# Keys by Strassen's half-size products from the fourth batch on, and their left blocks from DRAM

## The chip, the cores and the metric

The kernel runs on one core of a Trainium2 chip. The metric is the device time of one execution in microseconds; where several executions were timed, it is their median. A trace of one profiled execution of the kernel before is at hand.

## What is computed

Attention of eight batches of eight heads (512 local tokens with a window of 32, 32 global tokens, head size 64) is followed by a feed-forward part on all 576 tokens of a batch:

```python
x_prev = np.concatenate([np.zeros((B, 1, D), dtype=np.float32), x[:, :-1, :]], axis=1)
xk = mu_k * x + (1.0 - mu_k) * x_prev
xr = mu_r * x + (1.0 - mu_r) * x_prev
k = np.maximum(xk @ w_k, 0.0)
v = k * k @ w_v
r = 1.0 / (1.0 + np.exp(-(xr @ w_r)))
return (r * v).astype(np.float32)
```

Here x is the attention's output, of width 512; w_k is 512 x 1024, w_v 1024 x 512 and w_r 512 x 512, all in fp32. The three products are called keys, values and gates below.

## The kernel before, in words

Every fp32 matrix of the feed-forward part is split into a high and a low part, and a product of two matrices is made of three matmuls (high by high, high by low, low by high), written in `products` (L483 to L485). A matmul here has 128 x 128 weights and 256 columns. The low part of a split is made by a subtraction on POOL or DVE (L202, L517), the high part by a cast on ACT (L201, L516).

A batch has two halves of 256 tokens. For each, `mix` makes xk and xr (L508 to L517), `squares` makes keys and their squares: four groups of 24 matmuls, each into one bank, a relu on ACT (L549) and a multiplication on DVE (L551). `gates` makes the gates (L564, L566).

From batch 2 on (`FROM`), the values are made by Strassen's method for the two halves together: k squared is cut into four blocks B11, B12, B21, B22; `differences` makes T1 to T4 of them on DVE (L620); and seven half-size products take the place of eight (`values_1`, `values_2`, `product`, matmuls at L639). Their left blocks, parts of w_v and sums of them, lie in DRAM (`scratch`): `sums_of_values` makes them during batch 1 (stores at L231 and L245, additions and subtractions on POOL at L232 to L240), and `load_left` (L258) loads them into five buffers, two loads of 512 KB after each product of 24 matmuls. Sums of products are put together by copies of a bank on ACT (L657, L664, L674) and additions on DVE (L660, L673, L678, L685). The keys' weights wk_h and wk_l stay in SBUF all the time.

The heads' attention of the next batch runs beside the feed-forward steps of this one (`together`, `beside_heads`). Head scores are matmuls at L346 and L350, the softmax is L318 (DVE), L324 (ACT) and L334 (POOL), probabilities are transposed on TensorE (L371) and copied from PSUM at L373, by ACT for e = 0 and by DVE for e = 1. Nothing runs beside batch 7's feed-forward part and that of the global tokens: this is called the tail. The order of instructions on each engine is made by a scheduler when the kernel is built, from the order of the code, priorities and its own estimates; on the chip each engine and each queue then works strictly in that order. SP issues all DMA transfers, in order too.

The accumulators take PSUM banks in turn:

```python
MIDDLE_USE = {"m": [ps2, ps2, psx], "s": [ps4] * 4, "t": [ps1], "o": "s"}
```

## Time and profile before

| what | number |
|---|---|
| median of 3 runs | 703.33 us (700.31 to 703.79) |
| the profiled execution's own time | 702.47 us |
| its span in the trace | 700.6 us |
| mean granted TensorE clock | 0.978 |
| HBM read and written | 104.86 MB and 17.30 MB |
| loads of 768 KB of queries and keys, of 640 KB of v | 32 and 32 |

The profile's page gives busy time by engine, a view by stage gives it between two times, and a list of waits says what an idle engine was released by. Two lines of the page's slices, each a fortieth of the span, show how much of the start differs from the rest:

```profile
PE   4879989988999999999999999999999999999997
DMA  8732579462312452362909083635727090534665
```

A digit is the busy share in tenths (9 is 90% or more). Span times start at the first instruction; the batches' boundaries lie about 76 us apart from about 290 us on, and the last heads end at about 596 us.

### The profile page before, as it was taken

To read this page: it belongs to the slowest core of one execution; us is meant where nothing else is said; L and a number is where in the kernel's file an instruction comes from. 1 tells how busy PE (TensorE), PEld (TensorE's weight loads), DVE (VectorE), ACT (ScalarE), POOL (GpSimd) and SP (SyncE) were. 2 spreads that over 40 slices of the span, in tenths; PEclk is the share of its full clock that TensorE was granted. 3 is DMA by queue.
4 is the path that set the end of the run, shared out by engine and by line. 5 is a ranking of instruction groups with operands and counts; after the bars stand their busy time and mean duration, and the time that the engine had idled before them with its cause. 6 is when DMAs were issued, how large, how long until landed. Compare 5 with 4: busy or idle time off the path is not lost.

```text
span 700.6 us, 18622 instructions
## 1 busy us (share of the span) xinstructions
PE 667.4 (95%) x7472; PEld 629.2 (90%) x7472; DVE 417.7 (60%) x1217; ACT 387.9 (55%) x1058; POOL 357.2 (51%) x363
## 2 busy tenths in 40 slices
PE   4879989988999999999999999999999999999997
PEld 2658778978999999999999999999999999999996
DVE  5767977635635375645684557645674656477531
ACT  5756876447445456656557473757465643442530
POOL 5656597864524334573428353645348332642800
PEclk9659999999999999999999999999999999999999
DMA  8732579462312452362909083635727090534665
GB/s 344 288 99 109 200 215 338 157 237 80 127 71 92 132 216 76 122 242 75 359 20 338 25 312 140 222 140 175 279 89 274 2 352 11 196 121 166 216 189 198
DMA packets 43542, 123.37 MB, mean 176 GB/s; under 512 B 4032, under 2 KB 20928, under 8 KB 43456
## 3 DMA queue, kind: packets, MB, share of 16 engines
q1 hardware_dynamic: 43456, 122.18, 49.0%
q8 instruction: 59, 0.97, 0.6%
q14 instruction: 27, 0.22, 0.1%
HBM read 104.86 MB, written 17.30 MB: 174 GB/s over the span
## 4 chain that ended last, share of the span: by engine, by line
PE 75%; DMA 7%; POOL 6%; ACT 5%; DVE 4%; issue 2%; SPq 0%; POOLq 0%; ACTq 0%; DVEq 0%
PE ps_m L639 16%; PE ps_m L483 14%; PE ps_m L484 13%; PE ps_m L485 13%; PE ps_s L350 9%; DMA a<-scratch 3%; PE ps_t L371 3%; ACT Pt L324 2%; PE ps_s L352 2%; DMA w<-w_r 2%; DMA w<-w_v 1%; POOL Pt L334 1%; PE ps_t L421 1%; PE ps_t L350 1%; PE ps_t L380 1%
## 5 line engine op out<-in xcount | busy, mean ns | idle before, releaser
L483 PE MATMUL ps_m<-xkh,wk_h 128*128 128x256 f32 x544 | 155.4, 286 | 4.1 <-ACT xkh L516 2.8
L484 PE MATMUL ps_m<-xkl,wk_h 128*128 128x256 f32 x544 | 154.0, 283 | 0.4 <-POOL xkl L517 0.4
L485 PE MATMUL ps_m<-xkh,wk_l 128*128 128x256 f32 x544 | 153.8, 283 | 0.0
L639 PE MATMUL ps_m<-bh,a 128*128 128x256 f32 x736 | 139.5, 283 | 1.3 <-DMA a<-scratch 1.2
L324 ACT ACTIVATE Pt<-Pt,m 128x160 f32<-128x160 f32 x256 | 106.6, 419 | 26.7 <-DVE m L318 25.0
L639 PEld LDWEIGHTS ps_m<-bh,a 128*128 128x128 f32 x736 | 115.4, 188 | 4.0 <-issue 2.0
L483 PEld LDWEIGHTS ps_m<-xkh,wk_h 128*128 128x128 f32 x544 | 103.8, 191 | 6.1 <-ACT xkh L516 3.4
L334 POOL TENSOR_TENSOR Pt<-Pt,ssum 128x512 f32<-128x512 f32 x64 | 68.6, 1072 | 79.7 <-ACT xrh L516 23.2
L484 PEld LDWEIGHTS ps_m<-xkl,wk_h 128*128 128x128 f32 x544 | 103.9, 191 | 1.3 <-POOL xkl L517 0.7
L485 PEld LDWEIGHTS ps_m<-xkh,wk_l 128*128 128x128 f32 x544 | 103.7, 191 | 0.5 <-issue 0.2
L639 PE MATMUL ps_m<-bl,a 128*128 128x256 f32 x368 | 103.0, 280 | 0.0
L517 POOL TENSOR_TENSOR xkl<-xfull,xkh 128x512 fp32r<-128x512 f32 x34 | 46.9, 1379 | 99.3 <-ACT xkh L516 94.3
L483 PE MATMUL ps_m<-xrh,wr_h 128*128 128x256 f32 x272 | 78.4, 288 | 2.5 <-ACT relu L528 2.5
L551 DVE TENSOR_TENSOR B<-ps_m,relu 128x512 f32<-128x512 f32 x52 | 35.8, 689 | 74.6 <-ACT relu L549 74.5
L484 PE MATMUL ps_m<-xrl,wr_h 128*128 128x256 f32 x272 | 77.4, 285 | 0.0
L485 PE MATMUL ps_m<-xrh,wr_l 128*128 128x256 f32 x272 | 77.3, 284 | 0.0
L549 ACT ACTIVATE relu<-ps_m 128x512 f32<-128x512 f32 x52 | 31.0, 597 | 82.6 <-PE ps_m L485 82.6
L639 PEld LDWEIGHTS ps_m<-bl,a 128*128 128x128 f32 x368 | 69.2, 188 | 0.0
L318 DVE CUSTOM_DVE_ANT_0 Pt<-ps_s,masks 128x160 f32<-128x160 f32 x256 | 65.7, 317 | 2.6 <-PE ps_s L350 2.4
L586 POOL TENSOR_TENSOR gate<-sum,gate 128x512 f32<-128x512 f32 x18 | 26.7, 1481 | 59.3 <-DVE sum L685 38.4
L201 ACT CAST bh<-B 128x512 fp32r<-128x512 f32 x76 | 46.0, 620 | 18.2 <-PE ps_m L639 12.1
L483 PEld LDWEIGHTS ps_m<-xrh,wr_h 128*128 128x128 f32 x272 | 52.2, 192 | 3.2 <-ACT relu L528 2.6
(138 smaller groups left out, 1573.6 us busy)
## 6 DMA issues: line engine op xcount, KB each, us to landing
a<-scratch SPq DMA_DIRECT2D x92, 512.0 KB, 6.2
raw_qk<-qk SPq DMA_DIRECT2D x32, 768.0 KB, 5.5
raw_v<-v SPq DMA_DIRECT2D x32, 640.0 KB, 5.9
out_l<-gate SPq DMA_DIRECT2D x32, 256.0 KB, 4.6
w<-w_k SPq DMA_DIRECT2D x8, 512.0 KB, 9.7
w<-w_v SPq DMA_DIRECT2D x8, 512.0 KB, 4.5
w<-w_r SPq DMA_DIRECT2D x4, 512.0 KB, 4.0
scratch<-wv_h SPq DMA_DIRECT2D x8, 256.0 KB, 3.2
```

Source lines behind the costliest of these rows:

```text
L201: nc.scalar.copy(hi, val)
L318: read = nc.vector.tensor_tensor_reduce(out=Pt[:, i], in0=place(e, t, h), in1=masks[:, e, slots[t][1]], op0=ALU.add, op1=ALU.min, scale=-s ...
L324: nc.scalar.activation(Pt[:, i], Pt[:, i], AF.Exp, bias=low_x[:, i:i + 1], scale=-1.0, accum_out=ssum[:, i:i + 1],)
L334: nc.gpsimd.tensor_mul(out, Pt[:, each, at:at + n], rinv.unsqueeze(2).to_broadcast([P, 4, n]))
L350: self.last = nc.tensor.matmul(*a, **kw)
L483: nc.tensor.matmul(out, w_h[:, i, cols], x_h(i), start=(i == 0), stop=False)
L484: nc.tensor.matmul(out, w_h[:, i, cols], x_l(i), start=False, stop=False)
L485: nc.tensor.matmul(out, w_l[:, i, cols], x_h(i), start=False, stop=(i == n - 1))
L517: nc.gpsimd.tensor_sub(lo[:, both], xf, hi[:, both].bitcast(F32))
L549: nc.scalar.activation(rk, kp, AF.Relu)
L551: nc.vector.tensor_mul(k2[f0 // HC][f0 % HC // 2], kp, rk)
L639: nc.tensor.matmul(out[:, j], w, x[:, i % 2], start=fresh and (i, j, n) == (0, 0, 0), stop=(i, n) == (HC - 1, 2), skip_group_check=True,)
```

## The change

Keys of batches 3 to 7 are made by Strassen's method as well. `sums_of_keys` makes the left blocks of w_k during batch 2 and stores them in DRAM (`scratch_k`); wk_h and wk_l are then given up, and their room holds the split blocks of xk (`kxp`). The keys of a batch are two sets (n = 0, 1), each a `seven` with products of 12 matmuls and one left load of 512 KB each. `seven` serves keys and values; it takes three banks X, Y and Z and returns to X and Z for later products of the set. `Keys.mixed` makes the blocks T1 to T4 of xk: four subtractions on DVE, seven casts on ACT and seven low parts on POOL for a batch, in place of four casts and four low parts. Six buffers hold left blocks, in the tail six more tiles that the heads no longer use. The left blocks are loaded one by one, after each step of 12 matmuls: 170 loads instead of 92.

The sums of w_v's blocks move from every step of batch 1's feed-forward part to every other step of its second half, and wait for the last square of the batch's keys. The first chunks of weights are loaded into tiles of `mixp` and `gatep` instead of a pool of their own. From the fourth batch of heads on, both copies of transposed probabilities are by ACT (20 copies move). Gates are always evacuated with high priority. The keys of the global tokens are made from left blocks in DRAM too (`keys_of_one`). In the middle the steps beside a batch's heads are counted as 32 instead of 19.

```diff
-    MIDDLE_USE = {"m": [ps2, ps2, psx], "s": [ps4] * 4, "t": [ps1], "o": "s"}
+    MIDDLE_USE = {"m": [psa, psb, psx], "s": [ps4] * 4, "t": [ps1], "o": "s"}
...
+    gatew = ctx.enter_context(tc.tile_pool(name="gatew", bufs=1))
+    wr_h, wr_l = (gatew.tile([P, NC, NC * P], F32R, name=f"wr_{x}") for x in "hl")
+    keyu = ExitStack()
+    keyw = keyu.enter_context(tc.tile_pool(name="keyw", bufs=1, reuse_waits="tile"))
+    wk_h, wk_l = (keyw.tile([P, NC, DF], F32R, name=f"wk_{x}") for x in "hl")
...
+            home, tag = ((mixp, "mix"), (gatep, "gate"))[n // 2] if n < EARLY else (stage, "w64")
...
+    scratch_v = dramp.tile([P, len(LEFT), HC // 2, 2, 2, TOK], F32, name="scratch_v")
+    scratch_k = dramp.tile([P, len(LEFT), 2, 2, 2, TOK], F32, name="scratch_k")
...
+    def sums(home, tag, parts, out, first, after):
+        a = home.tile([P, 2, 2, TOK], F32, tag=tag, name="a")
+        hs, ls = (home.tile([P, 4, TOK], F32R, tag=tag, name=f"{x}s") for x in "hl")
+        for j in range(2):
+            for x in range(2):
+                behind(after, nc.sync.dma_start(out=out(2 * j, 2 * j + 2, x), in_=parts(x, j)))
+            add = first.tensor_add(a[:, j], parts(0, j), parts(1, j))
+            behind(after, add)
+        a11, a21, a12, a22 = (a[:, j, e] for j in range(2) for e in range(2))
...
+    def sums_of_keys():
+        for i in range(2):
+            for s in range(2):
+                sums(
+                    leftp, "a",
+                    lambda x, j: (wk_h, wk_l)[x][:, i + 2 * j].bitcast(F32)
+                    .rearrange("p (e s n) -> p s e n", e=2, s=2)[:, s],
+                    lambda lo, hi, x: scratch_k[:, lo:hi, s, i, x], nc.vector, Tokens.square,
...
+    SEVEN = (("A11", "B11"), ("A12", "B21"), ("S2", "T2"), ("S1", "T1"), ("S3", "T3"), ("S4", "B22"), ("A22", "T4"))
...
+    for b in range(FROM, B - 1):
+        plan(of_values, [a for a, _ in SEVEN])
+        plan(of_keys, [a for a, _ in SEVEN], True)
+    plan(of_keys, FOUR, True)
+    plan(of_values, [a for a, _ in SEVEN])
+    plan(of_values, ("A11", "A21", "A12", "A22"))
...
-        copy = nc.vector.tensor_copy if e else nc.scalar.copy
+        copy = nc.vector.tensor_copy if e and r.slots[0][0].b <= FROM else nc.scalar.copy
...
+                    xf = self.two(tmpp, "xfull") if hi is not None else blocks[c0 // 2]
...
+    def product(out, right, fresh=True):
+        for i, (b_h, b_l) in enumerate(right):
+            a, home = left.pop(0)
+            for c in range(2):
+                for j in range(2):
+                    a_h, a_l = (a[:, c, x, j * P:(j + 1) * P] for x in range(2))
+                    for n, (w, x) in enumerate(((a_h, b_h), (a_h, b_l), (a_l, b_h))):
+                        nc.tensor.matmul(
+                            out[:, j], w, x[:, c], start=fresh and (i, c, j, n) == (0, 0, 0, 0),
+                            stop=(i, c, n) == (len(right) - 1, 1, 2), skip_group_check=True,
+                        )
+            load_left(home)
+            yield
+    def new_bank():
+        return psum("m").rearrange("p (j n) -> p j n", j=2)
+    def seven(right, done):
+        X, Y, Z = new_bank(), new_bank(), new_bank()
+        if len(use["m"]) == 3:
+            turn["m"] -= 2
+        c11, u2, w = (sump.tile([P, 2, TOK], F32, tag="sum", name=name) for name in ("c11", "u2", "w"))
+        def add(bank, sum, *at):
+            with tc.high_priority():
+                nc.vector.tensor_add(sum, bank, sum)
+            done(*at, sum)
+        def copy(sum, bank):
+            with tc.high_priority():
+                nc.scalar.copy(sum, bank)
+        yield from product(X, right("B11"))
+        copy(c11, X)
+        yield from product(Y, right("B21"))
+        add(Y, c11, 0, 0)
+        yield from product(X, right("T2"), fresh=False)
+        copy(u2, X)
+        yield from product(Z, right("T1"))
+        copy(w, Z)
+        yield from product(X, right("T3"), fresh=False)
+        add(X, w, 1, 1)
+        yield from product(Z, right("B22"), fresh=False)
+        add(Z, u2, 0, 1)
+        yield from product(X, right("T4"), fresh=False)
+        done(1, 0, X)
...
+        def mixed(self):
+            B11, B21, B12, B22 = (self.xv[f"B{i}{j}"] for j in (1, 2) for i in (1, 2))
+            self.x_split("B11", B11)
+            self.x_split("B21", B21)
+            nc.vector.tensor_sub(B11, B12, B11)
+            nc.vector.tensor_sub(B12, B22, B12)
+            self.x_split("B22", B22)
+            nc.vector.tensor_sub(B22, B22, B11)
+            self.x_split("T2", B22)
+            self.x_split("T1", B11)
+            nc.vector.tensor_sub(B21, B21, B22)
+            self.x_split("T3", B12)
+            self.x_split("T4", B21)
+        def x_split(self, name, val):
+            self.x[name] = h, l = [Tokens.two(kxp, f"x{name}{x}", F32R, name + x) for x in "hl"]
+            split(val, h, l, nc.gpsimd)
...
+        def keys(self):
+            blocks = {(i, j): self.block(f"B{i + 1}{j + 1}") for j in range(2) for i in range(2)}
+            for n in range(2):
+                def done(i, j, v):
+                    if in_psum(v):
+                        rk = Tokens.two(tmpp, "relu")
+                        with tc.high_priority():
+                            nc.scalar.activation(rk, v, AF.Relu)
+                        with tc.high_priority():
+                            nc.vector.tensor_mul(blocks[i, j][n], v, rk)
+                    else:
+                        nc.vector.scalar_tensor_tensor(blocks[i, j][n], v, 0.0, v, op0=ALU.max, op1=ALU.mult)
+                yield from seven(lambda b: [self.x[b]], done)
...
+        def values(self):
+            def done(i, j, v):
+                self.tokens[j].write(i, v)
+            for n, _ in enumerate(seven(lambda b: self.parts.pop(b), done)):
+                if n == 4:
+                    self.split("T1", "T3", "B22", "T4")
+                yield
...
+        def keys_of_one(self):
+            t, = self.tokens
+            for i in (1, 2):
+                k = att2.tile([P, 8 * WG], F32, tag="Pt", name="k")[:, :HC * TOK]
+                k = k.rearrange("p (i n) -> p i n", n=TOK)
+                self.k[f"B{i}1"] = [k[:, 2 * n:2 * n + 2] for n in range(2)]
+            blocks = [self.k[f"B{i}1"] for i in (1, 2)]
+            halves = [[(t.xk_h[:, c:c + 2], t.xk_l[:, c:c + 2])] for c in (0, 2)]
+            for n in range(2):
+                for e in range(2):
+                    out = new_bank()
+                    yield from product(out, halves[0])
+                    yield from product(out, halves[1], fresh=False)
...
+            sums = sums_of_values()
+            for n, _ in enumerate(feed_forward(tokens_of(b), before)):
+                if n > FF_STEPS and n % 2:
+                    next(sums, None)
...
+                    keyu.close()
+                    kxp = ctx.enter_context(tc.tile_pool(name="kxp", bufs=1, reuse_waits="tile"))
+                    for _ in range(6):
+                        load_left()
...
+        this.mix(0)
+        for n, _ in enumerate(before.values()):
+            yield
+            if n == 4:
+                this.mix(1)
+            if n == 8:
+                this.mixed()
+        yield from this.tokens[0].gates()
+        if b == B - 1:
+            of_globals.tokens[0].mix()
+        yield from this.keys()
+        this.split("B11", "B21")
+        this.differences()
+        this.split("T2")
+        yield from this.tokens[1].gates()
...
+    for home in ((rawp, "qk", K0 + SK), (rawp, "v", NV), (att2, "PT", 8 * P)):
+        for _ in range(2):
+            load_left(home)
...
+        yield from of_globals.keys_of_one()
+        yield from last.values()
+        yield from of_globals.tokens[0].gates()
+        of_globals.split("B11", "B21")
+        yield from of_globals.values_of_one()
```

Three places show how the order of instructions changes. First the start: POOL, around the last two low parts of w_v's chunks (`wv_l`) and what stands between them and batch 1's mixes (`xkl`, `xrl`). Before:

```order
L202 TENSOR_TENSOR wv_l<-w_991,wv_h 128x512 [waits DMAHW7_49,Activation_49]
L232 TENSOR_TENSOR a<-wv_h,wv_l 128x512 [waits Pool_49]
L232 TENSOR_TENSOR a<-wv_h,wv_l 128x512
L334 TENSOR_TENSOR Pt<-Pt,ssum 128x4x128 [waits DVE_49,PE_49,Activation_49]
L334 TENSOR_TENSOR Pgl<-Pt,ssum 128x128 [waits PE_49]
L334 TENSOR_TENSOR Pt<-Pt,ssum 128x4x128 [waits Activation_49]
L334 TENSOR_TENSOR Pgl<-Pt,ssum 128x128
L237 TENSOR_TENSOR a<-a 128x256 [waits Pool_49]
L202 TENSOR_TENSOR wv_l<-w_1000,wv_h 128x512 [waits DMAHW2_49,Activation_49]
L202 TENSOR_TENSOR wv_l<-w_1112,wv_h 128x512 [waits DMAHW5_49,Activation_49]
```

`a` is a tile of sums. Now, from the same low parts on:

```order
L203 TENSOR_TENSOR wv_l<-w_994,wv_h 128x512 [waits DMAHW2_49,Activation_49]
L203 TENSOR_TENSOR wv_l<-w_1003,wv_h 128x512 [waits DMAHW3_49,Activation_49]
L381 TENSOR_TENSOR Pt<-Pt,ssum 128x4x128 [waits DVE_49,PE_49]
L381 TENSOR_TENSOR Pgl<-Pt,ssum 128x128 [waits PE_49]
L381 TENSOR_TENSOR Pt<-Pt,ssum 128x4x128
L381 TENSOR_TENSOR Pgl<-Pt,ssum 128x128
L203 TENSOR_TENSOR wv_l<-w_1115,wv_h 128x512 [waits DMAHW4_49,Activation_49]
L570 TENSOR_TENSOR xkl<-xfull,xkh 128x512 [waits PE_49,Activation_49]
L570 TENSOR_TENSOR xrl<-xfull,xrh 128x512 [waits PE_49,Activation_49]
```

The sums of w_v (now L242 to L249) are gone from this place; they stand further on, behind the last square (`k`) of batch 1's keys.

Second the middle: TensorE in the keys of batch 4. Before, a chain of products with the weights in SBUF, in which the heads' transposes stand:

```order
L483 MATMUL ps_m<-xkh,wk_h 128x256
L484 MATMUL ps_m<-xkl,wk_h 128x256
L485 MATMUL ps_m<-xkh,wk_l 128x256
L371 MATMUL ps_t<-ident,Pt 128x128 [waits Activation_49]
L371 MATMUL ps_t<-ident,Pt 128x128 x3
L483 MATMUL ps_m<-xkh,wk_h 128x256
L484 MATMUL ps_m<-xkl,wk_h 128x256
L485 MATMUL ps_m<-xkh,wk_l 128x256
```

Now, the second half of the product T2 and the start of T3, both in bank X; ACT copies the bank (`u2`) between them, and the first row of T3 waits for ACT (`Activation`):

```order
L649 MATMUL ps_m<-xT2h,a 128x256 x2
L649 MATMUL ps_m<-xT2l,a 128x256
L649 MATMUL ps_m<-xT2h,a 128x256
L649 MATMUL ps_m<-xT1h,a 128x256
L399 MATMUL ps_s<-raw_qk 64x160 [waits DMAHW7_49,DVE_49]
L397 MATMUL ps_s<-raw_qk 64x160 x15
L427 MATMUL ps_t<-ident,Pgl 128x128 [waits Activation_49]
L427 MATMUL ps_t<-ident,Pgl 128x128
L649 MATMUL ps_m<-xT3h,a 128x256 [waits DMAHW1_49,Activation_49]
L649 MATMUL ps_m<-xT3l,a 128x256
```

Between the last matmul of T2 and the first of T3 stand one matmul of T1 and the heads' scores. SP's queue in the same batches, with the loads of left blocks (`a`), of the heads' inputs and the stores of outputs, before:

```order
L258 DMA a<-scratch 128x1024 [waits DMAHW7_49,PE_49]
L710 DMA out_l<-gate 128x2x256 [waits DMAHW0_49,Activation_49,Pool_49]
L258 DMA a<-scratch 128x1024 [waits DMAHW1_49,PE_49]
L258 DMA a<-scratch 128x1024 [waits DMAHW4_49,DMAHW2_49,PE_49]
L710 DMA out_l<-gate 128x2x256 [waits DMAHW3_49,DVE_49]
L258 DMA a<-scratch 128x1024 [waits DMAHW5_49,PE_49]
L258 DMA a<-scratch 128x1024 [waits DMAHW6_49,PE_49]
L710 DMA out_l<-gate 128x2x256 [waits Pool_49]
L269 DMA raw_qk<-qk 128x1536 [waits DMAHW7_49,PE_49]
L269 DMA raw_qk<-qk 128x1536 [waits DMAHW0_49,PE_49]
```

And now:

```order
L305 DMA a<-scratch_v 128x1024 [waits DMAHW0_49,PE_49]
L305 DMA a<-scratch_v 128x1024 [waits DMAHW1_49,PE_49]
L305 DMA a<-scratch_v 128x1024 [waits DMAHW4_49,DMAHW2_49,PE_49]
L305 DMA a<-scratch_v 128x1024 [waits DMAHW5_49,DMAHW3_49,PE_49]
L305 DMA a<-scratch_v 128x1024 [waits DMAHW6_49,PE_49]
L316 DMA raw_qk<-qk 128x1536 [waits PE_49] x2
L305 DMA a<-scratch_v 128x1024 [waits DMAHW7_49,PE_49]
L321 DMA raw_v<-v 128x1280 [waits DMAHW0_49,PE_49]
L321 DMA raw_v<-v 128x1280 [waits DMAHW1_49,PE_49]
L305 DMA a<-scratch_v 128x1024 [waits DMAHW2_49,PE_49]
L305 DMA a<-scratch_v 128x1024 [waits DMAHW3_49,PE_49]
```

The heads' inputs stand behind more loads of left blocks, each of which waits for a product (`PE`) to free its buffer.

Third the end of the heads: POOL, from the last `Pg` of the heads on. Now:

```order
L455 TENSOR_SCALAR Pg<-Pg,ssumg 128x576 [waits DVE_49,Activation_49]
L203 TENSOR_TENSOR bl<-T_8759,bh 128x512 [waits PE_49,DVE_49,Activation_49,Pool_49]
L203 TENSOR_TENSOR xB11l<-xB_8842,xB11h 128x512 [waits PE_49,Activation_49]
L570 TENSOR_TENSOR xrl<-xfull,xrh 128x512 [waits Activation_49]
L203 TENSOR_TENSOR bl<-T_8759,bh 128x512 [waits Activation_49]
L203 TENSOR_TENSOR xB21l<-xB_8843,xB21h 128x512 [waits Activation_49]
L570 TENSOR_TENSOR xrl<-xfull,xrh 128x512 [waits Activation_49]
L203 TENSOR_TENSOR bl<-B_8396,bh 128x512 [waits PE_49,Activation_49]
L203 TENSOR_TENSOR bl<-B_8396,bh 128x512 [waits Activation_49]
L570 TENSOR_TENSOR xrl<-xfull,xrh 128x512 [waits Activation_49]
L203 TENSOR_TENSOR xT1l<-xB_8842,xT1h 128x512 [waits Activation_49]
L638 TENSOR_TENSOR gate<-c_8869,gate 128x512 [waits DMAHW4_49,DMAHW0_49,DVE_49]
```

The low parts of xk's blocks (`xB11l` and so on) stand between those of the values' blocks (`bl`) and of xr; before, POOL had the following from the second mix of batch 7 on:

```order
L202 TENSOR_TENSOR bl<-B_8363,bh 128x512 [waits Activation_49,Pool_49]
L202 TENSOR_TENSOR bl<-B_7830,bh 128x512 [waits PE_49,Activation_49]
L586 TENSOR_TENSOR gate<-sum,gate 128x512 [waits DMAHW4_49,DMAHW2_49,DVE_49]
L202 TENSOR_TENSOR bl<-B_7830,bh 128x512 [waits Activation_49]
L202 TENSOR_TENSOR bl<-B_7831,bh 128x512 [waits PE_49,Activation_49]
L517 TENSOR_TENSOR xkl<-xfull,xkh 128x512 [waits PE_49,Activation_49,Pool_49]
L517 TENSOR_TENSOR xrl<-xfull,xrh 128x512 [waits PE_49,Activation_49,Pool_49]
L517 TENSOR_TENSOR xkl<-xfull,xkh 128x512 [waits Activation_49]
L202 TENSOR_TENSOR bl<-B_7831,bh 128x512 [waits Activation_49]
L517 TENSOR_TENSOR xrl<-xfull,xrh 128x512 [waits Activation_49]
```

267 lines of the change are left out of this document (109 added, 158 removed).

## The prediction

> **What bounds the kernel now.** I read the page first: busy time, clock, and the engines' shares of the chain that ended last.
>
> ```profile
> span 700.6 us, 18622 instructions
> PE 667.4 (95%) x7472; PEld 629.2 (90%) x7472; DVE 417.7 (60%) x1217; ACT 387.9 (55%) x1058; POOL 357.2 (51%) x363
> PE 75%; DMA 7%; POOL 6%; ACT 5%; DVE 4%; issue 2%; SPq 0%; POOLq 0%; ACTq 0%; DVEq 0%
> ```
>
> TensorE is busy for 95% of the span, and the chain is mostly TensorE. An average hides stages, so the second view is busy time by stage, and the third the list of what TensorE waited for after 165 us.
>
> ```profile
> 165.00:240.00 75.00, 75.00 (x884) 71.22 (x884) 37.65 (x131) 40.38 (x120) 31.99 (x34) 1.00 0.25 89
> 408.00:484.00 76.00, 76.00 (x905) 72.97 (x902) 46.68 (x145) 44.82 (x127) 39.08 (x39) 1.00 0.52 190
> 484.00:560.00 76.00, 75.51 (x898) 72.60 (x898) 46.64 (x145) 44.74 (x127) 38.34 (x38) 1.00 0.48 173
> 596.00:648.00 52.00, 52.00 (x450) 51.97 (x448) 33.72 (x49) 22.29 (x40) 24.47 (x18) 1.00 0.48 162
> PE ps_m L639 <- DMA a<-scratch: 1.2, 3, 0.5
> ```
>
> The columns are length, busy time of PE, weight load, DVE, ACT and POOL, then clock, DMA share and GB/s. From 165 us on TensorE has no gap but 1.2 us; the middle batches repeat every 76 us with 47, 45 and 39 us of work on the other three engines. So here fewer matmuls are time, one for one, as long as nothing new makes TensorE wait.
>
> **Term 1: matmuls that go.** The keys of a batch were 192 matmuls of 256 columns (64 at each of L483, L484 and L485) and become two sets of seven products of 12, 168. Five batches change: 120 matmuls fewer. A matmul's listed 283 ns is its latency; what counts is the distance of starts, from these rows.
>
> ```profile
> 421.30 0.28 PE L483 MATMUL ps_m<-xkh,wk_h 128*128 128x256 f32 x1
> 423.92 0.28 PE L485 MATMUL ps_m<-xkh,wk_l 128*128 128x256 f32 x1
> 399.39 0.28 PE L483 MATMUL ps_m<-xrh,wr_h 128*128 128x256 f32 x1
> 401.78 0.28 PE L485 MATMUL ps_m<-xrh,wr_l 128*128 128x256 f32 x1
> 647.92 5.61 PE ps_m L639 x48
> ```
>
> The keys' first and last start enclose 23 distances: 2.62 / 23 = 0.1139 us. The gates' enclose 20: 2.39 / 20 = 0.1195. The products of the values take 5.61 / 48 = 0.1169. With keys at 0.1139 and the new products at 0.1169 a batch saves 21.87 − 19.64 = 2.23 us; with both at 0.1169, 2.81; with the new ones at the gates' pitch, 21.87 − 20.08 = 1.79. I take 2.5, five times: **−12.5 us**, between −9 and −14. The change does make the matmuls fewer: the order of the engine's instructions has 3816 of this form where it had 3936, and no other kind changes in number. That rules out the rival that it doesn't do what it says (702.5 us).
>
> **Term 2: the start.** The sums of the left blocks of w_v leave the stretch in which TensorE still waits.
>
> ```profile
> 115.00:120.00 5.00, 3.60 (x31) 3.37 (x30) 4.70 (x6) 1.15 (x4) 5.00 (x7) 1.00 0.96 313
> 145.00:150.00 5.00, 4.11 (x64) 3.36 (x62) 3.84 (x19) 3.40 (x16) 3.89 (x4) 1.00 0.75 258
> 150.00:155.00 5.00, 4.38 (x93) 4.07 (x97) 1.63 (x11) 0.87 (x2) 4.57 (x8) 1.00 0.97 320
> 155.00:160.00 5.00, 2.41 (x40) 1.78 (x40) 3.53 (x8) 2.56 (x6) 0.36 (x1) 1.00 1.00 379
> 160.00:165.00 5.00, 4.25 (x23) 4.04 (x24) 2.50 (x17) 4.89 (x20) 2.51 (x2) 0.71 0.29 102
> 161.89 0.42 PE L484 MATMUL ps_m<-xkl,wk_h 128*128 128x256 f32 x1
> 165.10 0.41 PE L484 MATMUL ps_m<-xkl,wk_h 128*128 128x256 f32 x1
> 153.26 0.69 POOL a L239
> 155.39 1.05 ACT hs L242
> ```
>
> From 145 to 165 us TensorE is idle for 0.89 + 0.62 + 2.59 + 0.75 = 4.85 us, and 15 distances in 3.21 us (0.214 us each) cost 15 × (0.214 − 0.114) = 1.5 us more; at 115 to 120 us 1.4 us are idle. On the chain lie POOL's sums and ACT's copy of them. Removing all would give 4.85 + 1.5 + 1.4 = 7.8 us. But the heads' own softmax chain comes next, and the other order of the first batches may cost as much as the windows above show in one place, 2.6 us. I take **−3 us**, range −7 to +3. The sums then run between about 165 and 240 us and those of the keys behind them, where POOL has 32 us of work in 75: nothing for them. The first chunks of weights in other tiles, and the copies of probabilities on ACT instead of DVE (below), are also at nothing.
>
> **Term 3: what the new form adds beside TensorE.** Rows by group:
>
> ```profile
> L373 DVE COPY PT<-ps_t 128x512 f32<-128x512 f32 x32 | 21.9, 685 | 25.3 <-PE ps_t L371 25.3
> L373 ACT COPY PT<-ps_t 128x512 f32<-128x512 f32 x32 | 18.8, 588 | 7.8 <-PE ps_t L371 7.8
> L620 DVE TENSOR_TENSOR B<-B,B 128x512 f32<-128x512 f32 x24 | 19.9, 829 | 0.2
> L685 DVE TENSOR_TENSOR sum<-ps_m,sum 128x512 f32<-128x512 f32 x6 | 4.1, 689 | 1.6 <-PE ps_m L639 1.4
> L551 DVE TENSOR_TENSOR B<-ps_m,relu 128x512 f32<-128x512 f32 x52 | 35.8, 689 | 74.6 <-ACT relu L549 74.5
> L549 ACT ACTIVATE relu<-ps_m 128x512 f32<-128x512 f32 x52 | 31.0, 597 | 82.6 <-PE ps_m L485 82.6
> L201 ACT CAST bh<-B 128x512 fp32r<-128x512 f32 x76 | 46.0, 620 | 18.2 <-PE ps_m L639 12.1 <-DVE B L551 3.5 <-POOL gate L586 1.5
> L202 POOL TENSOR_TENSOR bl<-B,bh 128x512 fp32r<-128x512 f32 x36 | 47.0, 1323 | 2.5 <-ACT bh L201 2.5
> L517 POOL TENSOR_TENSOR xkl<-xfull,xkh 128x512 fp32r<-128x512 f32 x34 | 46.9, 1379 | 99.3 <-ACT xkh L516 94.3 <-issue 5.0
> ```
>
> For a middle batch: DVE loses 4 copies (−2.7 us), 8 squares (−5.5) and L673's add (−0.7), and gains 4 differences (3.3), 6 adds and 8 squares of the two sets (9.6): 46.7 + 4.0 = 51 of 73.5 us. ACT gains 4 copies (2.4), 7 casts for 4 (1.9), 6 evacuations (3.5) and loses 6 relus (−3.6): 49 of 73.5. POOL gains 7 low parts for 4, 7 × 1.32 − 4 × 1.38 = 3.7: 43 of 73.5. None becomes the bound, so their sums cost nothing; their delays might.
>
> *Banks.* A product now goes back into a bank that a copy or add has just left: X, then Y or Z, then X again, four times in a set of seven, eight times a batch for keys, 40 in all. (In the values' sets the product between has 24 matmuls.) For keys it has 12: 12 × 0.1169 = 1.40 us, against 0.588 us for ACT's copy or 0.689 for DVE's add. The tightest place in the order (T3 behind T2) has not a whole product between, only one matmul and small head products. The evacuations are ahead of the rest by priority, yet must let the running instruction end (0.83 us for a difference). A wait is so between 0 and 0.689 + 0.83 + 0.23 − 1.40 = 0.35 us a time, with two matmul distances for the handover: 0 to 14 us in all. The old order's waits of this kind, the squares' among them, cost nothing after 165 us, so I stay near that end: **+2**.
>
> *Left blocks.* Each step of 12 matmuls now takes a 512 KB load; a middle batch has 28 instead of 14.
>
> ```profile
> a<-scratch SPq DMA_DIRECT2D x92, 512.0 KB, 6.2
> DMA to landing us min/median/max: 3.4/6.2/8.4
> 484.75 8.30 DMA a<-scratch
> 405.00:410.00 5.00, 5.00 (x107) 4.81 (x104) 0.89 (x7) 3.88 (x9) 5.00 (x7) 1.00 0.89 342
> 410.00:415.00 5.00, 5.00 (x66) 4.64 (x65) 3.82 (x5) 2.89 (x6) 2.26 (x3) 1.00 0.97 331
> 415.00:420.00 5.00, 5.00 (x43) 4.91 (x43) 3.91 (x20) 3.48 (x16) 1.21 (x1) 1.00 1.02 396
> 420.00:425.00 5.00, 5.00 (x46) 5.00 (x45) 2.27 (x6) 2.52 (x8) 2.74 (x3) 1.00 1.01 360
> 100.00:105.00 5.00, 3.06 (x21) 2.33 (x22) 3.11 (x6) 3.54 (x7) 3.68 (x4) 1.00 1.01 274
> ```
>
> Now 190 GB/s over 76 us are 14.4 MB a batch; 14 loads more are 7.3 MB, 21.8 in all. The four saturated rows average 357 GB/s, so the queue needs 61 of 73.5 us: busy, but not the bound. Six buffers give a load about five steps of 73.5 / 28 = 2.6 us, 13 us, against 6.2 to 8.4 for landing; behind heads' loads on SP's queue some have less. The old kernel paid 1.2 us for such cases; I take **+1.5**, from 0 to 6. In the tail a step of 1.40 us asks 374 GB/s, just over those rows, but gates and six more homes lie between: in the same term. At the heads' end POOL has 19 low parts nearly in a row, 19 × 1.32 = 25 us, which 28 steps of 1.40 us use one by one: **+0.5** (0 to 4).
>
> **Sum.** The profiled execution took 702.47 us (span 700.6): 702.5 − 12.5 − 3 + 2 + 1.5 + 0.5 = 691.0. The median of the runs shown is 703.33, 0.9 above it, and their range of 3.5 us is wider than that, so no correction.
>
> **A rule against it.** The row at 155 to 165 us shows what idling costs: TensorE busy for 2.41 of 5 us, then the clock 0.71. The next row shows a shorter wait that did no harm.
>
> ```profile
> 490.00:495.00 5.00, 4.51 (x52) 4.08 (x45) 4.23 (x21) 2.81 (x13) 1.77 (x1) 1.00 1.01 383
> ```
>
> The Trainium skill, "TensorE: Matmul & The Clock Gate", section "HAM oscillation — how this bites in real kernels", says that a slice of compute shorter than the wait for the next slice's data drops the clock at each slice, and "A second HAM failure mode: psum-queue depth-cycling" says the same of many short idles between groups that cycle through banks. By the first rule the time would be that of rival D. The trace agrees only for the long idle; half a microsecond at 493 us left the clock at 1.00.
>
> **Rivals.** A: *the start gains fully and no new wait appears*: 702.5 − 14 − 7 = 681.5. For it: no such wait cost anything after 165 us. Against: the rings are fuller than before.
> B: *ScalarE's and VectorE's copies hold the banks*: 40 times 0.35 us, 702.5 − 12.5 − 3 + 14 + 1.5 + 0.5 = 703. For it: both engines are two thirds busy, and one product is all the cover. Against: the mean evacuation is half of that cover.
> C, the slower side: *the loads pace the middle batches.* If the queues hold not 357 but the 274 GB/s of the row at 100 us, a batch takes 21.8 / 0.274 = 79.5 us instead of 76: four batches +14, and the tail's 58 loads (30.4 MB, some 29 after the ring's first) 106 us, 2 over the 104 that it has now: 702.5 − 3 + 14 + 2 = 715.5. It decides once the rate falls under 21.8 / 76 = 287 GB/s. Against: that row is of loads of weights among others; those of left blocks run at 331 to 396.
> D: *waits as long as at 155 us come once in each of ten sets*, 2.5 us idle and 1.5 for the clock: 691 + 40 = 731. It needs loads that land 2.5 us later than their cover.
>
> **Chances.** The forecast with its own bounds (685 to 698) 0.66, A 0.12, B 0.12 (two thirds of it within 0.5%), C 0.08, D 0.02. A measurement of this kernel can tell about 0.5% (3.5 us) from no change. Faster: 0.66 + 0.12 = 0.78, within: 0.09, slower: 0.13. The range leaves out a good half of A below and most of C and D with the upper part of B above: 683 to 703.
>
> **What would show it.** Right: starts of key products 0.114 to 0.120 us apart; the middle batches at 73 to 74 us; after 200 us waits of TensorE on ACT or DVE below 3 us and on loads below 3; DMA share about 0.8 in the middle; no sums of w_v on POOL ahead of 160 us and fewer idle microseconds there. Wrong: waits for ps_m's evacuations in every set (B), a DMA share of 1.0 with TensorE idle before each product (C), a clock under 1.00 after 200 us (D), or a start that ends later than 165 us.

## The result and the profile after

The changed kernel took 748.73 us (median of 4 runs, 747.78 to 750.29) beside 702.96 us for the kernel before (4 runs, 700.31 to 703.79): a ratio of 1.066, 95% interval 1.0625 to 1.0695. It is slower by 46 us; 12 us less had been forecast.

The page of the changed kernel, first its span, its busy times, the granted clock by slices and the engines' shares of the chain:

```profile
span 747.3 us, 18702 instructions
PE 684.1 (92%) x7352; PEld 638.0 (85%) x7352; DVE 496.0 (66%) x1249; ACT 406.3 (54%) x1097; POOL 418.1 (56%) x398
PEclk9659889999999999999997999979997999989999
PE 60%; DVE 21%; POOL 6%; ACT 6%; issue 4%; DMA 2%; SPq 0%; POOLq 0%; ACTq 0%; DVEq 0%
```

TensorE has 120 matmuls fewer and is busy longer. DVE's share of the chain went from 4% to 21%, and DVE is busy for 78 us more where the prediction had added 4 us a batch. The clock falls in slices far behind the start.

To see where, both spans are cut at the same points of the heads' work (starts of DVE's copies into xg_all, of which a batch's heads have two): batches 0 and 1, batch 2's feed-forward part with the sums, the four middle batches, the tail. Busy times by stage, the kernel before and then the changed one (length, then PE, PEld, DVE, ACT, POOL, clock, DMA share, GB/s):

```profile
0.00:226.90 226.90, 198.94 (x2241) 175.71 (x2243) 145.66 (x463) 138.36 (x401) 140.97 (x166) 0.93 0.51 181
226.90:297.70 70.80, 70.80 (x858) 67.27 (x855) 41.06 (x141) 40.30 (x119) 28.05 (x29) 1.00 0.38 137
297.70:594.10 296.40, 295.83 (x3494) 285.16 (x3492) 178.39 (x539) 170.13 (x470) 145.70 (x138) 1.00 0.50 181
594.10:700.60 106.50, 101.80 (x901) 101.04 (x897) 52.56 (x77) 39.15 (x68) 42.47 (x31) 1.00 0.54 178
```

```profile
0.00:225.80 225.80, 205.57 (x2240) 181.94 (x2241) 145.20 (x462) 137.44 (x400) 138.24 (x158) 0.90 0.50 177
225.80:312.00 86.20, 78.91 (x882) 73.90 (x880) 58.97 (x150) 48.36 (x131) 57.29 (x57) 0.96 0.72 246
312.00:633.70 321.70, 296.79 (x3384) 279.92 (x3383) 227.68 (x557) 178.44 (x494) 169.22 (x147) 0.95 0.76 257
633.70:747.30 113.60, 102.80 (x863) 102.27 (x859) 64.12 (x82) 42.10 (x73) 53.33 (x39) 0.95 0.71 253
```

The first stage is 1 us shorter, the second 15.4 longer, the middle 25.3, the tail 7.1. The cuts do not hold quite the same work: of the matmuls into ps_m 26 more lie ahead of the middle than before, the middle has 140 fewer where 96 go, the tail 6 fewer where 24 go. At 0.117 us each, some 3 us of the second stage's 15.4 are work that came later before (an estimate). What TensorE waited for behind 165 us (the line that waited, what released it, us in total, times, longest):

```profile
PE ps_t L418 <- ACT PTg L428: 12.1, 4, 6.8
PE ps_m L530 <- DVE c L669: 9.0, 2, 5.4
PE ps_m L649 <- ACT u L674: 6.9, 1, 6.9
PE ps_t L418 <- ACT PT L420: 3.5, 1, 3.5
PE ps_s L399 <- DVE xT L519: 2.7, 1, 2.7
PE ps_m L649 <- POOL bl L203: 2.6, 1, 2.6
PE ps_m L649 <- DMA a<-scratch_k: 1.2, 1, 1.2
```

Few waits, each long: near the start of each middle batch and of the tail lies a hole of one wait or two, 3.0, 6.8, 6.9, 7.0 and 6.9 us. Loads cost 1.2 us. The waits of 3.5 and 2.7 us lie in the second stage. The one at 399 us, engine by engine (start, duration, engine, line; in brackets the idle time before and its releaser), shows how it comes about:

```profile
390.07 0.48 DVE L563 SCALAR_TENSOR_TENSOR xfull<-diff,mu_r_sb,xT 128x256 f32<-128x256 f32 x1
391.14 1.53 DVE L563 SCALAR_TENSOR_TENSOR xB<-diff,mu_k_sb,xT 128x256 f32<-128x256 f32 x1
394.04 2.95 DVE L563 SCALAR_TENSOR_TENSOR xB<-diff,mu_k_sb,xT 128x256 f32<-128x256 f32 x2
396.91 2.93 DVE L563 SCALAR_TENSOR_TENSOR xfull<-diff,mu_r_sb,xT 128x256 f32<-128x256 f32 x2
400.37 0.68 DVE L669 TENSOR_TENSOR c<-ps_m,c 128x512 f32<-128x512 f32 x1
404.11 0.31 DVE L365 CUSTOM_DVE_ANT_0 Pt<-ps_s,masks 128x160 f32<-128x160 f32 x1
```

```profile
390.87 1.51 POOL L203 TENSOR_TENSOR bl<-T,bh 128x512 fp32r<-128x512 f32 x1 [2.39 <-ACT bh L202]
392.36 2.91 POOL L203 TENSOR_TENSOR bl<-B,bh 128x512 fp32r<-128x512 f32 x2
395.22 1.49 POOL L203 TENSOR_TENSOR xB21l<-xB,xB21h 128x512 fp32r<-128x512 f32 x1
396.67 1.47 POOL L570 TENSOR_TENSOR xrl<-xfull,xrh 128x512 fp32r<-128x512 f32 x1
```

```profile
399.88 0.62 ACT L569 CAST xrh<-xfull 128x512 fp32r<-128x512 f32 x1 [4.11 <-DVE xfull L563]
405.77 0.35 ACT L428 COPY PTg<-ps_t 128x256 f32<-128x256 f32 x1
```

```profile
406.17 1.11 PE L418 MATMUL ps_t<-ident,Pt 128*128 128x128 f32 x4 [6.80 <-ACT PTg L428]
400.00:410.00 10.00, 3.83 (x19) 3.61 (x19) 9.79 (x26) 6.58 (x23) 7.05 (x5) 0.59 0.36 112
```

For 2.4 us up to 390.9 POOL is idle, and a mix on DVE takes 0.48 us. From then on POOL runs low parts without a break, and the same instruction takes 1.5 us: one of DVE's for each of POOL's. The six mixes from 391.14 on take until 399.77, 8.6 us in place of some 2.4 at 0.4 us from start to start: DVE falls behind by about 6 us there. ACT's queue stands for 4.1 us at a cast that needs DVE's result; DVE's masks of the heads' scores begin at 404; ACT's copy PTg stands behind both, and TensorE waits 6.8 us for it. In the ten us around it the clock is at 0.59. The sum c (L669), for which TensorE waits elsewhere, stands behind the mixes in the same way.

### The profile page after: what moved, and what is told of

Same layout as the page of the kernel before. It is cut to its first block, busy times and chain, and to the rows that moved or that the text cites. A ratio compares the mean times of both kernels' runs of the same rounds, so it can differ in the third digit from the quotient of the medians.

```text
span 747.3 us, 18702 instructions
## 1 busy us (share of the span) xinstructions
PE 684.1 (92%) x7352; PEld 638.0 (85%) x7352; DVE 496.0 (66%) x1249; ACT 406.3 (54%) x1097; POOL 418.1 (56%) x398
## 4 chain that ended last, share of the span: by engine, by line
PE 60%; DVE 21%; POOL 6%; ACT 6%; issue 4%; DMA 2%; SPq 0%; POOLq 0%; ACTq 0%; DVEq 0%
PE ps_m L649 26%; PE ps_s L397 7%; PE ps_m L531 6%; PE ps_m L530 6%; PE ps_m L532 6%; DVE xfull L563 5%; DVE diff L559 4%; DVE xB L563 4%; ACT Pt L371 3%; PE ps_t L418 2%; PE ps_t L393 2%; PE ps_s L399 1%; DVE Pt L365 1%; POOL a L242 1%; PE ps_t L468 1%
## 5 line engine op out<-in xcount | busy, mean ns | idle before, releaser
L202 ACT CAST bh<-B 128x512 fp32r<-128x512 f32 x72 | 44.2, 620 | 29.3 <-DVE B L740 15.1
L418 PE MATMUL ps_t<-ident,Pt 128*128 128x128 f32 x256 | 43.7, 300 | 16.7 <-ACT PTg L428 12.1
L530 PE MATMUL ps_m<-xkh,wk_h 128*128 128x256 f32 x192 | 57.8, 304 | 0.4 <-ACT gate L616 0.4
L531 PE MATMUL ps_m<-xkl,wk_h 128*128 128x256 f32 x192 | 56.8, 297 | 0.2 <-POOL xkl L570 0.2
L532 PE MATMUL ps_m<-xkh,wk_l 128*128 128x256 f32 x192 | 55.7, 291 | 0.0
L532 PEld LDWEIGHTS ps_m<-xrh,wr_l 128*128 128x128 f32 x272 | 53.9, 198 | 1.9 <-issue 1.8
L531 PEld LDWEIGHTS ps_m<-xrl,wr_h 128*128 128x128 f32 x272 | 54.0, 198 | 1.7 <-issue 1.4
L570 POOL TENSOR_TENSOR xrl<-xfull,xrh 128x512 fp32r<-128x512 f32 x34 | 48.4, 1425 | 11.6 <-ACT xrh L569 11.6
L203 POOL TENSOR_TENSOR bl<-B,bh 128x512 fp32r<-128x512 f32 x36 | 50.9, 1425 | 5.2 <-ACT bh L202 5.2
L563 DVE SCALAR_TENSOR_TENSOR xfull<-diff,mu_r_sb,xT 128x256 f32<-128x256 f32 x64 | 49.9, 797 | 5.5 <-POOL xkl L570 5.5
L559 DVE TENSOR_TENSOR diff<-xT 128x256 f32<-128x256 f32 x64 | 45.5, 748 | 11.5 <-ACT xT L522 11.5
```

Source lines behind the costliest of these rows:

```text
L203: engine.tensor_sub(lo, val, hi.bitcast(F32))
L418: nc.tensor.transpose(tp[:, i], r.Pt[:, 4 * e + i, SG * e:SG * e + W], ident)
L530: nc.tensor.matmul(out, w_h[:, i, cols], x_h(i), start=(i == 0), stop=False)
L531: nc.tensor.matmul(out, w_h[:, i, cols], x_l(i), start=False, stop=False)
L532: nc.tensor.matmul(out, w_l[:, i, cols], x_h(i), start=False, stop=(i == n - 1))
L559: nc.vector.tensor_sub(self.shape(diff[:, j]), self.cur(c0 + j), self.prev(c0 + j))
```

## The experiments

The theory (1): DVE's operations on two SBUF operands take turns with POOL's instructions; where both are dense, the queues stop and TensorE idles and slows. Rivals: (2) DVE has too much work ahead of what TensorE waits for, with or without POOL; (3) the loads; (4) the copies of probabilities on ACT. Each kernel is the changed one but for the edit shown, unless another is named. A time without a ratio is that of one execution; the four of the changed kernel lie within 2.5 us.

**Low parts of xk's blocks on DVE.**

```diff
-            split(val, h, l, nc.gpsimd)
+            split(val, h, l, nc.vector)
```

> The seven low parts of xk's blocks a batch are made by DVE instead of POOL. Theory 1 (DVE's operations on two SBUF operands stand still while POOL runs an instruction, ACT's queue stands behind their results, TensorE idles and its clock falls): POOL loses 7 x 1.42 us a batch, so the mixes' operations drop from about 1.1 us towards 0.42 to 0.48, and at least 15 of the 46 us go: 725 to 733 us. Theory 2 (DVE simply has too much work placed ahead of what TensorE waits for, with or without POOL): DVE gains 7 x 0.69 us a batch and the time rises to 750 to 760. Theory 3 (loads of left blocks) and theory 4 (copies of probabilities on ACT): no change, 745 to 752.

746.97 us beside 701.89: neither theory 1's number nor theory 2's, but inside the range for no change (theories 3 and 4). The low parts of the values' blocks and of xr on POOL still met the mixes, and the low parts moved to DVE are such operations themselves. Of this run, DVE:

```profile
476.18 1.77 DVE L203 TENSOR_TENSOR xB21l<-xB,xB21h 128x512 fp32r<-128x512 f32 x1
477.87 1.52 DVE L563 SCALAR_TENSOR_TENSOR xB<-diff,mu_k_sb,xT 128x256 f32<-128x256 f32 x1
480.74 0.47 DVE L563 SCALAR_TENSOR_TENSOR xB<-diff,mu_k_sb,xT 128x256 f32<-128x256 f32 x1
```

**Half of each left block loaded.** The sum over c uses the same half of the left block twice.

```diff
-            nc.sync.dma_start(out=part.bitcast(F32), in_=src)
+            nc.sync.dma_start(out=part.bitcast(F32)[:, 0], in_=src[:, 0])
...
-                    a_h, a_l = (a[:, c, x, j * P:(j + 1) * P] for x in range(2))
+                    a_h, a_l = (a[:, 0, x, j * P:(j + 1) * P] for x in range(2))
```

> Each load of a left block brings 256 KB instead of 512, and both halves of the sum over c use the same left half: the products are those of wrong blocks, with as many matmuls. Theory 3 (loads pace the products or hold up SP's queue): 700 to 725 us. Theories 1, 2 and 4: within 1% of the changed kernel, 742 to 755.

747.15 us. Theory 3 falls: 44 MB less moved nothing.

**Copies of probabilities back on DVE.**

```diff
-        copy = nc.vector.tensor_copy if e and r.slots[0][0].b <= FROM else nc.scalar.copy
+        copy = nc.vector.tensor_copy if e else nc.scalar.copy
```

> The copies of transposed probabilities for e = 1 are made by DVE for all batches, as before the change. Theory 4 (TensorE waits for copies that ACT does late): the waits of L418 for ACT go and the time falls to 715 to 735 us. Theory 1: ACT's copies are late because ACT stands behind casts that wait for DVE, so the waits stay or move, 742 to 760. Theory 2: DVE gains 20 x 0.685 us, 750 to 762. Theory 3: no change.

748.68 us: theory 4 falls, and the term of nothing for these copies was right. The waits moved to DVE's copy; of this run:

```profile
PE ps_t L427 <- DVE PT L420: 24.3, 5, 7.3
```

**Sums of left blocks on DVE** (the four lines of additions and subtractions, and the first addition of w_v's).

```diff
-        nc.gpsimd.tensor_add(a22, a21, a22)
+        nc.vector.tensor_add(a22, a21, a22)
...
```

> All additions and subtractions of the sums of left blocks are made by DVE instead of POOL; they run between 165 and 300 us, where the changed kernel loses about 14 us against the one before. Theory 1: POOL loses 8 x 3.2 + 8 x 1.39 us = 37 us of work there, most of these 14 us come back: 735 to 740 us. Theory 2: DVE has 25 to 30 us more there, 752 to 765 us. Theories 3 and 4: no change.

742.65 us, 6 less; the second stage is 75.5 us long in place of 86.2, but the first is 3 longer, so the direction is theory 1's, and the gain is short of its range.

**The mix later in the code.**

```diff
-            if n == 4:
+            if n == 8:
                 this.mix(1)
-            if n == 8:
+            if n == 12:
                 this.mixed()
```

> The second half's mix and the differences of xk's blocks stand four steps later beside the values (steps 8 and 12 in place of 4 and 8). Theory 1 in its second form (POOL's instructions and DVE's operations on two SBUF operands run one after the other, so that what counts is the sum of both, and a burst of both stops the queues): the same sum in longer time, each of the holes of 5 to 7 us shrinks by a third or more: 728 to 740 us. Theory 2 (place of DVE's work alone): the same sign, 720 to 740. If it stays at 745 to 752, the place is not what counts.

748.31 us, and it tells nothing on places: in the traces of the two kernels every engine has the same order of instructions. A place in the code is not a place in a queue here.

**Low parts left out**, first those of xk's blocks, then those of the blocks of k squared as well.

```diff
-            self.x[name] = h, l = [Tokens.two(kxp, f"x{name}{x}", F32R, name + x) for x in "hl"]
-            split(val, h, l, nc.gpsimd)
+            h = Tokens.two(kxp, f"x{name}h", F32R, name + "h")
+            self.x[name] = h, h
+            nc.scalar.copy(h, val)
...
-                    h, l = (Tokens.two(mlp, f"b{x}", F32R, tag) for x, tag in zip("hl", tags))
-                    split(val, h, l, nc.vector if b[0] == "B" else nc.gpsimd)
-                    self.parts[b].append((h, l))
+                    h = Tokens.two(mlp, "bh", F32R, tags[0])
+                    nc.scalar.copy(h, val)
+                    self.parts[b].append((h, h))
```

> The seven low parts of xk's blocks a batch are left out, on POOL and DVE alike; the products use the high part twice, with as many matmuls. Theory 1: 9.9 us a batch leave POOL and nothing comes to DVE, so the sum of both falls from about 70 to 60 us of a batch's 80 and the holes in the middle go by half or more: 715 to 732 us. Theory 2: DVE keeps its operations and their place, 742 to 752.

> As the run before, and the low parts of the blocks of k squared are left out too (eight on POOL and six on DVE a batch), with the high part used twice. Matmuls, loads, banks, copies and the evacuations stay. Theory 1: nearly all of the loss behind 300 us is gone; with the 12.5 us of matmuls saved and the 14 us that the sums cost before 300 us left, 700 to 712 us. If banks, loads or the place of the mixes were the cause, it stays above 730.

738.67 and 709.09 us. The first lies between the ranges of theories 1 and 2: the low parts of the values' blocks and of xr on POOL still met the mixes. The second is within theory 1's range, but it takes six low parts a batch from DVE too, so it does not part theory 1 from theory 2; a run below does. Middle and tail of the second run:

```profile
310.00:601.80 291.80, 284.75 (x3351) 269.23 (x3349) 171.99 (x534) 179.24 (x495) 88.85 (x90) 1.00 0.83 283
601.80:707.30 105.50, 101.33 (x897) 100.74 (x891) 40.16 (x69) 41.47 (x72) 23.76 (x18) 1.00 0.77 274
```

With the same banks and loads the middle is 30 us shorter and the clock at 1.00. Middle and tail together, which hold the same matmuls in both kernels but for one, take 397.3 us in place of 435.3. TensorE's idle time there fell from 24.9 + 10.8 = 35.7 to 11.2 us, and its busy time by 13.5 us while the clock rose from 0.95 to 1.00: for the same matmuls, that part is put down to the clock.

**Only the sums moved, in the kernel before.**

```diff
...
-            for _ in feed_forward(tokens_of(b), before):
-                next(sums, None)
+            for n, _ in enumerate(feed_forward(tokens_of(b), before)):
+                if n > FF_STEPS and n % 2:
+                    next(sums, None)
...
```

As in the change, the sums also wait for the last square of batch 1's keys.

> The kernel before, with only the sums of w_v's blocks moved to the second half of batch 1 behind the last square, on POOL as they are. If the term of the start was right (3 us in the changed kernel's first 165 us) and the sums cost nothing where they go: 698 to 701 us. Theory 1: the sums meet the mixes between 165 and 260 us and cost there what they gain: 701 to 710 us.

701.67 beside 704.12 us, ratio 0.9966 (0.9943 to 0.999): a gain of about 2.4 us (0.7 to 4.0 by the interval), near the 3 of the prediction's term. The time itself lies 0.7 us inside the range that was named for theory 1, so it does not decide whether these sums cost something where they go.

**All low parts on DVE, then with the sums on DVE too.** Three places: both calls of split in Keys, and the low part of xr in mix from the fourth batch on.

```diff
-                    nc.gpsimd.tensor_sub(lo[:, both], xf, hi[:, both].bitcast(F32))
+                    (nc.vector if blocks else nc.gpsimd).tensor_sub(lo[:, both], xf, hi[:, both].bitcast(F32))
...
-                    split(val, h, l, nc.vector if b[0] == "B" else nc.gpsimd)
+                    split(val, h, l, nc.vector)
```

> From the fourth batch on all low parts of the feed-forward part (of xk's blocks, of xr, of the blocks of k squared) are made by DVE; POOL keeps the softmax's products, the gates' products and the sums. POOL loses some 17 x 1.42 us a batch, DVE gains 17 x 0.69. Theory 1 (POOL and DVE's operations on two SBUF operands take turns; where both are dense, DVE goes at POOL's pace): with POOL thin, DVE's operations run at their own 0.42 to 0.69 us, most holes go: 715 to 732 us. Theory 2 (DVE has too much work in front of what TensorE waits for): DVE gains 12 us a batch, 755 to 775 us.

> The run before together with the sums of left blocks on DVE, which alone gave 6 us: under theory 1 the two add up, 708 to 726 us. If it comes under 700 it would beat the kernel before; I give that one chance in ten.

708.44 us, 40 less than the changed kernel, below even theory 1's range. Theory 2 falls: more was put on DVE. The second: 709.7 us, ratio 1.0087 (1.0059 to 1.0116), so the sums on DVE add nothing more to it; why they gave 6 us alone is open. Middle and tail of the first:

```profile
310.50:602.60 292.10, 286.44 (x3395) 271.56 (x3393) 223.57 (x629) 180.90 (x495) 72.74 (x74) 1.00 0.83 285
602.60:706.20 103.60, 99.78 (x861) 99.46 (x857) 62.75 (x106) 42.57 (x73) 20.55 (x14) 1.00 0.77 277
```

In this first run, the place that was shown at 399 us in the changed kernel:

```profile
388.00 0.87 DVE L563 SCALAR_TENSOR_TENSOR xfull<-diff,mu_r_sb,xT 128x256 f32<-128x256 f32 x2
393.68 0.32 DVE L365 CUSTOM_DVE_ANT_0 Pt<-ps_s,masks 128x160 f32<-128x160 f32 x1
391.37 3.55 POOL L638 TENSOR_TENSOR gate<-c,gate 128x512 f32<-128x512 f32 x1 [15.37 <-DVE c L669]
```

The mix still stands ahead of the heads' masks in DVE's queue, now with six low parts among it, but POOL is idle for 15.4 us and a mix takes under 0.5 us. From the mix's first difference to the masks pass 10.0 us, where the changed kernel needs 15.1.

**The second half's mix held behind POOL's low parts**, by a dependence; nothing changes its engine.

```diff
-                    split(val, h, l, nc.vector if b[0] == "B" else nc.gpsimd)
+                    low = split(val, h, l, nc.vector if b[0] == "B" else nc.gpsimd)
+                    if b[0] == "T":
+                        Keys.low = low
...
-            self.tokens[half].mix([self.xv[name] for name in names])
+            self.tokens[half].mix([self.xv[name] for name in names], Keys.low if half else None)
...
-                    nc.vector.tensor_sub(self.shape(diff[:, j]), self.cur(c0 + j), self.prev(c0 + j))
+                    d = nc.vector.tensor_sub(self.shape(diff[:, j]), self.cur(c0 + j), self.prev(c0 + j))
+                    if hold is not None:
+                        behind(hold, d)
```

> The second half's mix is held, by a dependence, behind the last low part of the values' blocks T3, T1, T4 on POOL, so that it can't run beside them; all operations stay on their engines. Theory 1, in the form that it is the meeting of the mix with POOL's low parts that stops the queues: the holes shrink, 725 to 742 us. If the sum of both engines' work counts and not their meeting: 743 to 755 us.

712.97 us: 36 less, for one dependence, and again below theory 1's range. The middle:

```profile
310.60:601.80 291.20, 287.57 (x3384) 272.22 (x3382) 209.50 (x557) 179.22 (x494) 168.42 (x147) 0.99 0.84 284
```

POOL has the same 168 us of work there, DVE 18 us less of the same instructions. The hold also puts the mix behind the masks of the heads in DVE's queue; this run can't part the two, but the run with all low parts on DVE can: it has no hold, the mix stands ahead of the masks, and what is gone is POOL's work. Other meetings remain in the run with the hold: three of the four differences of xk's blocks still take 1.41 to 1.46 us on the mean, where one alone takes 0.68, and TensorE does not idle for them. So a meeting costs only where the queues have no slack for it.

**More of POOL, in the kernel before.**

```diff
-                    split(val, h, l, nc.vector if b[0] == "B" else nc.gpsimd)
+                    split(val, h, l, nc.gpsimd)
```

> The kernel before, with the six low parts a batch that DVE makes (of the blocks B11, B21, B22) made by POOL: no Strassen keys, no further loads, banks as before. POOL gains 6 x 1.4 us a batch and DVE loses 6 x 0.69. Theory 1: DVE's mixes meet POOL more often, TensorE gets holes of the same kind and the clock falls: 708 to 730 us. If the holes of the changed kernel need its banks, loads or new order, nothing happens here: 699 to 706 us.

703.82 us: theory 1's number was wrong here. POOL's additional low parts lie where hardly a mix runs (between 411 and 427 us, for one batch, with mixes up to 404 and from 436 on), and the mixes keep their means of 0.65 and 0.54 us. So more work on POOL does nothing by itself; it is the meeting, at a place without slack, that counts.

**A version to beat both.** The held mix with the sums of w_v at the first steps of batch 1 as before the change and those of w_k in its second half; that with all low parts on DVE; and the latter without the hold.

```diff
-            sums = sums_of_values()
+            sums, sums_k = sums_of_values(), sums_of_keys()
             for n, _ in enumerate(feed_forward(tokens_of(b), before)):
+                next(sums, None)
                 if n > FF_STEPS and n % 2:
-                    next(sums, None)
+                    next(sums_k, None)
...
```

> The held mix, and the sums of w_v at the first steps of batch 1 as before, those of w_k in batch 1's second half (built in the buffers of the chunks of weights). Theory 1: batches 2's mixes no longer meet the sums, some 8 to 13 us of the 13 lost before 311 us come back, the middle stays at 73 us a batch: 699 to 706 us. If the loss there is not the sums': 710 to 715 us.

> The run before with all low parts of the feed-forward part on DVE from the fourth batch on. Theory 1: POOL is thin in the middle and the tail, and the tail takes 103.6 us as in the run with the low parts alone: 692 to 702 us, more likely than not under the kernel before.

> The low parts on DVE and the sums moved, without the held mix. Theory 1: with POOL thin the meeting of mix and low parts costs little, so within 4 us of the run before: 694 to 706 us.

709.99 us (ratio 1.0096, 1.0074 to 1.0117), 700.36 us (0.9961, 0.9942 to 0.998) and 705.16 us (1.0015, 0.9991 to 1.0039), each beside 704.06. The first is above its range of 699 to 706. The second is the fastest form of the change, and 0.4% faster than the kernel before: its interval lies below 1, but the gain is under the 0.5% that the prediction took as the least to be told from no change. The third differs from the second in the hold alone and takes 4.8 us more; what the hold does there was not traced further. Stages of the second:

```profile
0.00:227.70 227.70, 199.01 (x2245) 175.84 (x2247) 161.43 (x474) 141.99 (x404) 154.02 (x177) 0.95 0.60 209
227.70:301.80 74.10, 72.17 (x862) 68.28 (x858) 43.16 (x144) 43.22 (x124) 27.57 (x30) 1.00 0.48 171
301.80:594.20 292.40, 287.57 (x3402) 272.73 (x3400) 238.92 (x631) 181.02 (x496) 79.28 (x75) 1.00 0.83 286
594.20:697.90 103.70, 99.86 (x861) 99.54 (x857) 63.19 (x106) 42.92 (x73) 20.85 (x14) 1.00 0.77 277
```

The second stage has gone from 86.2 to 74.1 us. What the sums' place is worth is read from two runs that differ in it alone, both with the held mix (the sums' buffers differ too): the second stage goes from 86.3 to 73.8 us, of which some 4 us are matmuls that now come later (37 fewer into ps_m, an estimate), but the first from 224.3 to 229.8, and the whole gains 3 us (712.97 to 709.99). So the place caused about 8 of the 12 us lost in that stage beyond the work moved into it, and elsewhere the sums cost some 5 us again. The first run of the three kept POOL's low parts and its tail is 110.8 us long: the tail's loss is POOL's too.

## Why the prediction was wrong

*Term 1, the matmuls,* was right in size, as far as distances of starts show it; the stages' busy times do not, since they hold different work. The new key products start 1.28 / 11 = 0.116 us apart, by these rows of the changed kernel (12 matmuls from the first to the last), where 0.1169 was taken:

```profile
452.54 0.28 PE L649 MATMUL ps_m<-xT1h,a 128*128 128x256 f32 x1
453.82 0.27 PE L649 MATMUL ps_m<-xT1h,a 128*128 128x256 f32 x1
```

Over all pairs of them that follow each other directly the mean is 0.1165; that of the keys before, from 297 us on, is 0.1154, so the 0.1139 of the prediction's rows was a low one. 192 × 0.1154 − 168 × 0.1165 = 2.6 us a batch, where 2.5 was taken.

*Term 2, the start,* was right in size (2.4 us in the kernel before with the sums moved; the first stage is 1.1 us shorter in the changed kernel, 2.1 and 2.6 in the runs without low parts and with the held mix, which have the same start). The term was wrong in what followed: "nothing for them" was said of the sums behind 165 us because POOL had 32 us of work in 75. With those of the keys, their place cost about 8 us in the second stage.

*Term 3 holds the step that failed:* "None becomes the bound, so their sums cost nothing; their delays might." It took each operation's mean duration as a constant of its kind and added up each engine by itself. For DVE that gave 51 us a middle batch; the changed kernel has 227.68 / 4 = 56.9, and with the mix held 209.50 / 4 = 52.4. DVE's mixes are not constant: these rows, minimum, median and maximum in ns, are of the changed kernel.

```profile
L563 DVE SCALAR_TENSOR_TENSOR xB<-diff,mu_k_sb,xT x40: 464/480/1537, 295.0 to 649.3; 128x256 f32<-128x256 f32 x40
L559 DVE TENSOR_TENSOR diff<-xg_all x4: 1399/1494/1536, 654.1 to 665.6; 128x256 f32<-128x256 f32 x4
L669 DVE TENSOR_TENSOR c<-ps_m,c x16: 676/685/693, 307.9 to 712.7; 128x512 f32<-128x512 f32 x16
```

The sum c, with one operand in PSUM, never takes longer; the mixes do. Their spread by a factor of more than three stood in the trace of before, in the same kind of row, and was not looked at:

```profile
L512 DVE SCALAR_TENSOR_TENSOR xfull<-diff,mu_k_sb,xT x64: 468/476/1526, 32.9 to 619.1; 128x256 f32<-128x256 f32 x64
L508 DVE TENSOR_TENSOR diff<-xT x64: 406/419/1536, 32.2 to 618.3; 128x256 f32<-128x256 f32 x64
```

The change put both halves' mixes beside the values' products, where POOL makes their low parts, and added seven low parts of xk's blocks to the same place. The Trainium skill, "SBUF — State Buffer", section "Who interferes with whom", says that a DVE instruction with two SBUF inputs contends with a GpSimd instruction that reads SBUF, and that the ports they share are an exclusive lock. The rows agree: 0.48 us alone and 1.5 beside POOL's low parts, and 0.68 to 0.69 at all times with one operand in PSUM. This section of the Trainium skill would have been the rule against the change.

*Left blocks (+1.5)* were right: 1.2 us of waits for loads in the changed kernel, and no change with half the loads. *Banks (+2)* were right too: in the run without low parts TensorE waits 2.2 us for ACT's copies of banks (u and w). The longer waits of the changed kernel for u and c are no price of the banks, since they are gone in the runs where POOL's low parts are gone. *The tail (+0.5)* was wrong for the same cause: it lost 7.1 us, and with the low parts on DVE it takes 103.6 us, 2.9 less than before.

*The rivals.* A, B and C did not come. D named idle time with the clock behind it, and that came, at a chance of 0.02: 24.5 us of idle time and 13.5 us for the clock in the middle and the tail. But D put the idle time down to late loads; it was a mix on DVE. That the clock falls behind a long idle time, as the prediction read from the row at 155 to 165 us, is borne out by the row at 400 to 410 (6.8 us idle, 0.59); waits of 1.5 us and less, in the middle of the run without low parts, left it at 1.00.

Open: with the holes healed the middle takes 291 to 292 us, not the 286 that the matmuls alone would give; in the run without low parts 7.0 us of idle time are left, in waits of 1.5 us and less, most of them for ACT.

## What to carry to other kernels

Before moving work between stages, look at the minimum and maximum of each DVE operation and at what POOL does beside the slow ones; DVE's spare time counts only where POOL leaves it its full speed. Where a scheduler orders by its own estimates, one dependence that keeps DVE's mixes from POOL's low parts (and puts them behind the masks) was worth 36 us here; moving lines of code, in the one try, was worth nothing. A long hole on TensorE costs more than its own length, because the clock falls behind it: 24.5 us of holes went with 13.5 us of slower matmuls.
